# Layer norm, attention and a squared-ReLU gate on one core: another order at three borders

## The chip, the cores and the metric

The kernel runs on one core of a Trainium2 chip. The metric is the device time of one execution in microseconds (us); the median of three runs is compared. A profile is one further execution, whose span runs from the first to the last instruction.

The engines are named as the profile names them: PE (TensorE) does matmuls, PEld is its weight load, DVE is VectorE, ACT is ScalarE, POOL is GpSimd, and SP is SyncE, which here only issues DMAs. PE writes its results to PSUM, which has eight banks of 128 x 512 float32.

## The reference

```
xn = layernorm(x)                            # x: 2048 x 640
q  = xn @ wq                                 # 32 heads of 128
k, v = last 512 rows of k_cache, v_cache     # 32 heads, 512 x 128 each
p  = softmax(q @ k.T * 128**-0.5)            # per head, 2048 x 512
s  = concat(p @ v) @ wo                      # 2048 x 640
h  = relu(xn @ w1 + b1) ** 2                 # w1: 640 x 1728
g  = silu(h @ w2 + b2)                       # w2: 1728 x 640
out = x + s * g
```

Everything is float32. The kernel reaches this precision with three matmuls per product: each operand is split into a high part (rounded by ACT to the type that PE multiplies) and a low part (the rest, one subtraction), and high x high, high x low and low x high are added up in PSUM. So every operand costs one ACT operation, one DVE or POOL operation, and every 128 x 128 x 512 product three matmuls.

## The kernel before, in words

**MLP.** The 2048 tokens are four tiles of 512. F = 1728 is 13 chunks of 128 and one of 64, which stands as chunk 3. `mlp_step(n)` goes over (tile, chunk) for tiles 0 to 2: `up(t, f)` (15 matmuls, `ph`), then relu on ACT, square on POOL, the high part on ACT and the low part on DVE (`h`), and, one step later, `down` of the chunk before (15 matmuls into five banks `py`). So PE does up(f + 1) between up(f) and down(f). After a tile, `gate` writes the sigmoid gate to DRAM (`g_d`).

Tile 0 is made by `ln_first`: four blocks of x are loaded, normalised and turned by 20 PE transposes (`px`), behind 32 transposes of the identity (`pw`, `WARM`). The biases come through POOL's DMA queue (`br`) and are turned by one transpose (`pb`) that stands on PE ahead of those of x. During tile 0 the weights are read and split too: `load_w(f)` reads and splits chunk f ahead of `up(0, f)`; chunks 1 and 2 are read early into spare buffers. The statistics of tile t + 1 are made in one go at chunk 5 of tile t (`ln_stats`; chunk 3 for the last tile), its normalised chunks from chunk 9 (7) on. Instructions made through `pe`, `dve`, `act`, `pool` and `sp` keep the program's order; those made through `nc.` may be moved by the scheduler.

**Attention.** A unit is one head and one tile of 512 tokens: 128 units, in two halves of two tiles each. A hand-written plan (`at`, `on`) gives each step a due time in units of `PERIOD`; the steps are then issued in the order of these times. In unit i PE does the four score groups `s` (12 matmuls) into the four `s` banks, the query of unit i + 2 (`pq`, 15), the values of unit i - 1 (`o`, 12) and, for a finished pair of heads, the output projection (`r`, 15 per unit). The softmax of a unit: `max_fold` on DVE for each score bank (`rdm`), `gather` on ACT, `row` on DVE (`rowm`), a store of the maxima to DRAM (`m_d`) and a broadcast load of them (`bm`), both on SP; then `shift` on DVE (`e`), which empties the score banks, `expo` and `p_hi` on ACT, `p_lo` and the sum `su` on POOL. The sums take a like way (`rds`, `rows`, `s_d`, `bs`), and `o_norm`, `o_hi` and `o_lo` make `ot` from the one `o` bank. `pq` and `r` share two banks.

**Borders.** The last tile's MLP is done within attention. Its chunks 11 to 13 (`FA = FC - 3`) are multiplied by `early_up` (`eu`) in units 0 to 3, where there is no `r` yet; `late_relu`, `late_square` and `early_split` make their high and low parts, which go to DRAM (`h_d`). The other chunks run behind the last unit (`lu`, `ly`), with the three early ones last, five gates and the last stores. At the start of the second half, the two new tiles of xT are loaded in 20 pieces by SP (`load_xT`, `ax`), and each finished piece of the first half is stored at once (`s_d<-acc`).

Of the kernel before, what the change touches and what calls it, by code (L numbers as in the profile page):

```python
# [14 lines left out]
P = 128  # L15
NT = 512
EPS = 1e-5
WARM = 32
# [3 lines left out]
def kernel(  # L22
# [65 lines left out]
    h_d = {f: dpool.tile([P, 2, NT], F32, name=f"h_d{f}") for f in range(FC - 3, FC)}  # L88
# [13 lines left out]
    FA = FC - 3  # L102
# [10 lines left out]
    for f, (f0, n) in enumerate(chunks):  # L113
        wp = wpa if f < FA else wpb
        if n < P:
            w1s.append([wp.tile([P, DC, 2 * n], F32R, name=f"w1s{f}")])
        else:
            if f < FA - 1:
# [12 lines left out]
    def ln_tile(t, b):  # L131
        tag = "stage" if t or b < 2 else "mr"
        return xp.tile([P, D], F32, tag=tag, name=f"xb{t}_{b}")

    def ln_stats(t):
        mv = xp.tile([P, 4, NB], F32, tag="mv", name=f"mv{t}")[:, :2, :]
        sc = xp.tile([P, 3, NB], F32, tag="sc", name=f"sc{t}")
        sts = [
            xp.tile([P, 2, 6], F32, tag="st", name=f"st{t}_{b}", bufs=4) for b in range(NB)
        ]  # L140
        xn = []
        for b in range(NB):
# [3 lines left out]
            xn.append(xb)  # L146
        hd = D // 2
        for b in range(NB):
            for i in range(2):
                dve.bn_stats(sts[b][:, i, :], xn[b][:, i * hd : (i + 1) * hd])  # L150
            dve.bn_aggr(mv[:, :, b], sts[b])
        var, sd, y = (sc[:, i, :] for i in range(3))
        r = mv[:, 1, :]
        dve.tensor_scalar(var, r, EPS, None, op0=ALU.add)
        nc.scalar.activation(sd, var, AF.Sqrt)
# [5 lines left out]
        xs = [  # L161
            keep.tile([P, DC, NT], F32R, tag="acc", name=f"xT{t}_{i}", bufs=2)
            if t % 2
            else xp.tile([P, DC, NT], F32R, tag=f"xT{i}", name=f"xT{t}_{i}", bufs=1)
            for i in range(2)
        ]
        return mv, xs

    def ln_rows(t, mv, xs):
# [7 lines left out]
        for i in range(2):  # L177
            m = xp.tile([P, D], F32, tag="mr", name=f"mr{t}_{i}")[:, :NT]
            nc.sync.dma_start(m, d[i : i + 1, :].to_broadcast([P, NT]))
            bc.append(m)  # L180
        return bc, xs
# [9 lines left out]
    PRE = {}  # L191

    def ln_first():
# [7 lines left out]
        pool.memset(warm, 1.0)  # L201
        act.activation(warm, warm, AF.Sqrt)
# [7 lines left out]
        dve.memset(br, 0.0)  # L210
        for lo, hi in ((0, rp), (rp, rp + 1), (rp + 1, FC)):
# [4 lines left out]
        pool.dma_start(br[32 : 32 + DC, :], b2.rearrange("(c p) -> c p", p=P))  # L216
        raws = load_w_raw(0)
        PRE.update({f: load_w_raw(f, True) for f in (1, 2)})
# [3 lines left out]
        pb = ps_h.tile([P, NT], F32, tag="ph", name="pb")  # L222
        pe.transpose(pb[:, :P], br, ident)
# [15 lines left out]
        def newton(k, eng):  # L239
            sign = -1.0 if k == 0 else 1.0  # L240
            eng.tensor_tensor(R[k], Y[k], Y[k], op=ALU.mult)
            eng.tensor_tensor(R[k], R[k], VAR[k], op=ALU.mult)
            eng.tensor_scalar(R[k], R[k], -0.5 * sign, 1.5 * sign, op0=ALU.mult, op1=ALU.add)
            eng.tensor_tensor(R[k], R[k], Y[k], op=ALU.mult)
# [23 lines left out]
        newton(0, pool)  # L268
# [9 lines left out]
        split_hi(0, raws, 0)  # L278
        dve.reciprocal(Y[1], SD[1])
        newton(1, dve)  # L280
# [10 lines left out]
        dve.tensor_copy(b1_sb, pb[:, :FC])  # L291
        dve.tensor_copy(b2_sb, pb[:, 32 : 32 + DC])
        pool.tensor_copy(warm, xn[NB - 1][:, D - 1 :])
        split_lo(0, raws, 0, pool)
# [3 lines left out]
        split_hi(1, PRE[1], 0)  # L298
        split_lo(1, PRE[1], 0, pool)
        split_hi(0, raws, 1)  # L300
        split_lo(0, raws, 1, dve)
# [6 lines left out]
    def load_w_raw(f, early=False):  # L308
        f0, n = chunks[f]
        if early:  # L310
            two = keep.tile([P, 2, D], F32, tag="acc", name=f"wr{f}", bufs=2)
            wa, wb = two[:, 0, :].rearrange("p (c n) -> p c n", n=P), two[:, 1, :]
        else:
            wa = xp.tile([P, DC, P], F32, tag="stw", name=f"w1r{f}", bufs=2)
        nc.sync.dma_start(
            wa[:, :, :n], w1[:, f0 : f0 + n].rearrange("(c p) f -> p c f", p=P)
        )
        if not early:
            wb = xp.tile([P, D], F32, tag="stw", name=f"w2r{f}", bufs=2)
        for k in range(0, P, n):  # L320
            nc.sync.dma_start(wb[k : k + n, :], w2[f0 : f0 + n, :])
        return wa[:, :, :n], wb
# [7 lines left out]
    def split_hi(f, raws, k, engine=act):  # L330
        engine.activation(split_parts(f, k)[0], raws[k], AF.Copy)

    def split_lo(f, raws, k, engine):
        hi, lo = split_parts(f, k)
        engine.tensor_tensor(lo, raws[k], raw(hi), op=ALU.subtract)

    def load_w(f):
        if f == 1:
            parts = ((1, 1), (2, 0))
        elif f == 2:  # L340
            parts = ((2, 1),)
        else:
            parts = ((f, 0), (f, 1))
        raws = PRE.get(f) or load_w_raw(f)
        for m, k in parts:
            if f < 3:
                split_hi(m, PRE[m], k)
                split_lo(m, PRE[m], k, dve)
            else:
# [782 lines left out]
```

## Time and profile before

| | |
|---|---|
| runs | 1979.35, 1977.17, 1979.55 us; median 1979.35 |
| profiled execution | 1980.79 us, span 1979.0 us |
| instructions | 25665, of these 8608 matmuls |
| PE busy | 1959.6 us, 99% of the span |
| DVE, POOL, ACT busy | 77%, 70%, 60% |
| mean granted TensorE clock | 0.998 |
| DMA | 220.35 MB, 111 GB/s over the span |

Matmuls are pipelined: a row's mean time of one (about 390 ns) is longer than the distance between two starts, and the busy time of PE counts the ends as the profile models them. A loss on PE is therefore read best from how many matmuls a stretch holds against its length.

### The profile page before, as it was taken

The numbers are of one execution on the slowest core, as the hardware profiler recorded it, in microseconds if no ns is written. First come the engines' busy times: TensorE is split into PE (matmuls) and PEld (weight loads), VectorE is DVE, ScalarE is ACT, GpSimd is POOL, SyncE is SP. The second block draws the span as 40 slices with busy tenths as digits, with TensorE's granted clock in tenths as the row PEclk, the third lists the DMA queues.
The fourth block names the chain that finished last, engine by engine and source line by source line (L and its number), as shares of the span: only waits on it lengthen the run. The fifth ranks groups of instructions, "written<-read, shape, count | busy, mean of one in ns | idle before, by whom it ended". The sixth has DMA issues, their size and how long they took to land.

```text
span 1979.0 us, 25665 instructions
## 1 busy us (share of the span) xinstructions
PE 1959.6 (99%) x8608; PEld 1611.1 (81%) x8608; DVE 1530.7 (77%) x2639; ACT 1188.1 (60%) x2039; POOL 1378.9 (70%) x763
## 2 busy tenths in 40 slices
PE   9999999999999999999999999999999999999998
PEld 7888887788888888888887778888888888888887
DVE  6433337788888888888887778888888888888864
ACT  5332336766666666666665676666666666666643
POOL 2121226888888888888887778888888888888841
PEclk9999999999999999999999999999999999999999
DMA  5331453333323223323335433333333333233454
GB/s 169 105 118 27 181 198 131 102 91 93 92 93 92 91 91 91 91 91 92 93 96 165 156 99 107 112 112 113 115 110 115 114 112 113 97 91 91 110 150 139
DMA packets 128917, 220.35 MB, mean 111 GB/s; under 512 B 23590, under 2 KB 38352, under 8 KB 127504
## 3 DMA queue, kind: packets, MB, share of 16 engines
q1 hardware_dynamic: 125792, 204.28, 34.5%
q0 software_dynamic: 2992, 14.43, 1.8%
q8 instruction: 67, 1.10, 0.2%
q14 instruction: 66, 0.54, 0.1%
HBM read 194.26 MB, written 24.39 MB: 110 GB/s over the span
## 4 chain that ended last, share of the span: by engine, by line
PE 79%; DVE 7%; DMA 6%; ACT 5%; issue 2%; POOL 1%; SPq 0%; ACTq 0%; POOLq 0%; DVEq 0%
PE r L73 18%; PE pq L73 18%; PE o L73 14%; PE s L73 14%; PE ph L391 6%; DMA bm<-m_d 2%; DVE e L73 2%; DMA m_d<-rowm 2%; PE py L97 2%; PE py L98 2%; PE py L96 2%; PE ly L73 2%; ACT e L73 1%; DVE rdm L73 1%; DVE acc L73 1%
## 5 line engine op out<-in xcount | busy, mean ns | idle before, releaser
L73 POOL TENSOR_TENSOR pt<-e,pt 128x1024 fp32r<-128x1024 f32 x256 | 616.4, 2408 | 130.8 <-ACT pt L73 105.0
L73 PE MATMUL r<-ot,wo 128*128 128x512 f32 x1920 | 497.0, 389 | 0.2 <-DVE acc L73 0.2
L73 PE MATMUL pq<-ax,wq 128*128 128x512 f32 x1920 | 456.5, 389 | 0.9 <-DMA ax<-xT_d 0.8
L73 PEld LDWEIGHTS pq<-ax,wq 128*128 128x128 f32 x1920 | 360.4, 188 | 76.3 <-DMA ax<-xT_d 1.7
L73 PEld LDWEIGHTS r<-ot,wo 128*128 128x128 f32 x1920 | 360.2, 188 | 75.8 <-DVE acc L73 0.6
L73 PE MATMUL s<-q,wk 128*128 128x512 f32 x1536 | 370.3, 390 | 5.0 <-DVE e L73 5.0
L73 PE MATMUL o<-pt,wv 128*128 128x512 f32 x1536 | 372.5, 391 | 2.0 <-DVE ot L73 1.4
L73 ACT ACTIVATE e<-e 128x1024 f32<-128x1024 f32 x256 | 269.7, 1053 | 140.6 <-DVE e L73 119.1
L73 DVE TRANSPOSE_TENSOR_REDUCE rdm<-s 128x16 f32<-128x512 f32 x512 | 342.8, 707 | 1.4 <-PE s L73 1.3
L73 PEld LDWEIGHTS s<-q,wk 128*128 128x128 f32 x1536 | 287.6, 188 | 68.3 <-DVE e L73 8.2
L73 PEld LDWEIGHTS o<-pt,wv 128*128 128x128 f32 x1536 | 286.8, 188 | 68.0 <-DVE ot L73 5.0
L73 DVE TENSOR_TENSOR e<-s,bm 128x512 f32<-128x512 f32 x512 | 312.6, 666 | 22.4 <-DMA bm<-m_d 22.2
L73 POOL TENSOR_TENSOR su<-e,e 128x1024 f32<-128x1024 f32 x128 | 308.0, 2406 | 0.0
L73 ACT ACTIVATE pt<-e 128x1024 fp32r<-128x1024 f32 x256 | 271.8, 1062 | 7.8
L73 DVE TENSOR_TENSOR acc<-r,acc 128x512 f32<-128x512 f32 x300 | 203.0, 677 | 8.8 <-PE r L73 8.5
L354 POOL TENSOR_TENSOR r<-r 128x512 f32<-128x512 f32 (+1 forms) x42 | 44.1, 1049 | 209.9 <-ACT r L399 190.9
L73 ACT ACTIVATE ot<-o 128x512 fp32r<-128x512 f32 x128 | 76.7, 599 | 172.3 <-DVE o L73 172.3
L73 DVE TRANSPOSE_TENSOR_REDUCE rds<-su 128x32 f32<-128x1024 f32 x128 | 158.3, 1237 | 1.6 <-POOL su L73 1.6
L73 DVE TENSOR_TENSOR ot<-o,ot 128x512 fp32r<-128x512 f32 x128 | 88.6, 692 | 85.2 <-ACT ot L73 85.2
L391 PE MATMUL ph<-xT,w1s 128*128 128x512 f32 x585 | 139.3, 390 | 0.0
L73 ACT ACTIVATE q<-pq 128x512 fp32r<-128x512 f32 x128 | 76.7, 599 | 101.2 <-PE pq L73 100.9
L73 POOL TENSOR_TENSOR wq<-qr,wq 128x640 fp32r<-128x640 f32 x62 | 97.8, 1577 | 56.5 <-ACT wq L73 56.5
(131 smaller groups left out, 2026.5 us busy)
## 6 DMA issues: line engine op xcount, KB each, us to landing
bm<-m_d SPq DMA_DIRECT2D x128, 256.0 KB, 3.3
bs<-s_d SPq DMA_DIRECT2D x128, 256.0 KB, 3.9
qr<-in_wq_dram SPq DMA_DIRECT2D x64, 320.0 KB, 4.3
or<-in_wo_dram SPq DMA_DIRECT2D x64, 320.0 KB, 4.2
kr<-in_kT_dram SPq DMA_DIRECT2D x64, 256.0 KB, 3.3
vr<-in_v_dram SPq DMA_DIRECT2D x64, 256.0 KB, 4.2
xT_d<-xT POOLq DMA_DIRECT2D x6, 1280.0 KB, 7.5
xb<-in_x_dram SPq DMA_DIRECT2D x16, 320.0 KB, 3.3
```

The lines of the kernel that those rows point to most:

```text
L73: ins = method(*args, **kwargs)
L96: nc.tensor.matmul(ps, ah, bh, start=first and i == 0, stop=False)
L97: nc.tensor.matmul(ps, ah, bl, start=False, stop=False)
L98: nc.tensor.matmul(ps, al, bh, start=False, stop=last and i == n - 1)
L354: nc.gpsimd.tensor_tensor(r, r, r, op=ALU.mult)
L391: nc.tensor.matmul(ph, w1s[f][i][:, c, :], xs[j][:, c, :], start=k == 0, stop=k == len(order) - 1,)
```

## The change

- **Start and first tile.** `WARM` is 36. The bias loads go through SP, behind the two weight loads of chunk 0, and `biases()` turns them behind the tenth matmul of `up(0, 0)`. `root` takes the square root with the epsilon as its bias; `newton` has three DVE steps for the second pair of blocks. `load_part(f, k)` reads w1 (k = 0) or w2 (k = 1) of a chunk two chunks ahead up to chunk 9, one ahead after that. `split_w(f, 1)` stands ahead of `up(0, f)`, `split_w(f + 1, 0)` behind the square of chunk f. Tile 0 uses the ordered engines. The statistics of tile 1 are loaded at chunk 1, made at chunks 2 to 5 (`ln_block`), and finished by `ln_var` and `ln_root`.
- **Border to attention.** `FA = FC - 4`: chunk 10 is done early as well. Its product stands where the query of unit 1 stood, and that query goes into unit 0 with the one of unit 2. `early_square` squares from PSUM in one operation; the square alone goes to DRAM, and `late_hs` splits it at the end.
- **Units.** The second `p_hi` stands behind the next unit's gather. From unit 4 on, `o` of even units uses the spare bank.
- **Border between the halves.** `load_xT` is issued by ACT at other times, `store_acc` is a step of its own one to three units later. `finish` is cut into `finish_gate` and `finish`.

The core of the diff:

```
-WARM = 32
+WARM = 36
...
-    FA = FC - 3
+    FO, FA = FC - 3, FC - 4
...
-            pool.dma_start(
+            sp.dma_start(
                 br[lo:hi, :m], b1[f0 : f0 + m * (hi - lo)].rearrange("(f p) -> f p", p=m)
             )
...
-        pb = ps_h.tile([P, NT], F32, tag="ph", name="pb")
-        pe.transpose(pb[:, :P], br, ident)
...
         def root(k):
+            act.activation(SD[k], R[k], AF.Sqrt, bias=eps)
             dve.tensor_scalar(VAR[k], R[k], EPS, None, op0=ALU.add)
-            act.activation(SD[k], VAR[k], AF.Sqrt)
...
+    def split_w(f, k):
+        if f < FC:
+            split_hi(f, PRE[f, k], k)
+            split_lo(f, PRE[f, k], k, dve)
+            if 9 <= f < FC - 1:
+                load_part(f + 1, k)
...
+    def square_split(t, f, r, hi, lo):
+        g, a, v = engines(t)
+        g.tensor_tensor(r, r, r, op=ALU.mult)
+        if t == 0 and f:
+            split_w(f + 1, 0)
+        a.activation(hi, r, AF.Copy)
+        v.tensor_tensor(lo, r, raw(hi), op=ALU.subtract)
...
+            if t == f == 0 and k == 9:
+                biases()
...
             if t == 0 and f > 0:
-                load_w(f)
+                split_w(f, 1)
+                if f < 8:
+                    for k in range(2):
+                        load_part(f + 2, k)
...
-            QPS[i] = bank(f"pq{i}", int(i != 1))
+            QPS[i] = bank(f"pq{i}", 1)
...
-            PO[i] = pools["psb"].tile([P, NT], F32, tag="o", name=f"o{i}", bufs=1)
+            if i % 2 or i < UPG:
+                PO[i] = pools["psb"].tile([P, NT], F32, tag="o", name=f"o{i}", bufs=1)
+            else:
+                PO[i] = psx.tile([P, NT], F32, tag="x", name=f"o{i}")
...
-        if g == NG - 1 and hf == 0:
-            sp.dma_start(s_d[t][:, d, :], ACC[hf, t][:, d, :])
+
+    def store_acc(t, d):
+        sp.dma_start(s_d[t][:, d, :], ACC[0, t][:, d, :])
...
+    def early_square(f):
+        r = LR[f]
+        dve.scalar_tensor_tensor(
+            r, LPH.pop(f), b1_sb[:, f : f + 1], r, op0=ALU.add, op1=ALU.mult
+        )
...
-    q_mm(1, range(DC))
-    q_hi(1)
-    q_lo(1)
+    EARLY_IN = (-1,) * 5 + (0,) * 4 + (1,) * 4 + (2,) * 4 + (3,) * 3
+    EARLY = [(FA + n // DC, n % DC) for n in range(len(EARLY_IN))]
+    for (f, c), u in zip(EARLY, EARLY_IN):
+        if u < 0:
+            early_up(f, 0, c)
...
-            w = (NG * UPG + t * G - 3 - AHEAD + t + k) * PERIOD + (8.5 if late else -1.6)
...
+        w = (NG * UPG + t * G - 5) * PERIOD
+        X_AT = [(11.65, 2)]
+        for k in (1, 2):
+            X_AT += [(k * PERIOD + 3.97, 2), (k * PERIOD + 7.85, 1)]
+            X_AT += [(k * PERIOD + 11.65, 2)] * (k == 1)
...
+                at(w + when, load_xT, 1, t, i, slice(c, c + 1), act)
...
+        qs = [(i + AHEAD, 3.45 if i % G and i > UPG else 4.3, 4.1)]
+        if i == 0:
+            qs = [(1, 2.8, 4.1), (2, 9.1, PERIOD - 5.2)]
+        elif i < UPG:
+            qs = [(i + 2, 4.9 if i == 3 else 4.2, 4.1)]
...
-        on(14.8, p_hi, i, 1)
+        on(PERIOD + 4.0, p_hi, i, 1)
...
-    EARLY_IN = (0,) * 7 + (1,) * 3 + (2,) * 3 + (3,) * 2
```

More of the change, by code (lines that the diff above doesn't have):

```diff
@@ L160, in ln_stats, with ln_rows @@
         dve.tensor_tensor(r, r, y, op=ALU.mult)
[L161 to L169, printed above, removed]
+        return mv
+    def ln_rows(t, mv):
         pm = psx.tile([P, NT], F32, tag="x", name=f"pmv{t}")
@@ L180, in ln_rows @@
             bc.append(m)
+        xs = [
+            keep.tile([P, DC, NT], F32R, tag="acc", name=f"xT{t}_{i}", bufs=2)
+            if t % 2
+            else xp.tile([P, DC, NT], F32R, tag=f"xT{i}", name=f"xT{t}_{i}", bufs=1)
+            for i in range(2)
+        ]
         return bc, xs
@@ L306, in spill, with load_part @@
             pool.dma_start(xT_d[t][i][:, cs, :], raw(xs[i])[:, cs, :])
[L308 removed]
+    def load_part(f, k):
         f0, n = chunks[f]
[L310 to L322 removed]
+        if f % 3 and f < 9:
+            if k == 0:
+                BOTH[f] = keep.tile([P, 2, D], F32, tag="acc", name=f"wr{f}", bufs=2)
+            w = BOTH[f][:, k, :]
+        else:
+            w = xp.tile([P, D], F32, tag="stw", name=f"w{k + 1}r{f}", bufs=2)
+        if k == 0:
+            w = w.rearrange("p (c n) -> p c n", n=P)[:, :, :n]
+            sp.dma_start(w, w1[:, f0 : f0 + n].rearrange("(c p) f -> p c f", p=P))
+        else:
+            for i in range(0, P, n):
+                sp.dma_start(w[i : i + n, :], w2[f0 : f0 + n, :])
+        PRE[f, k] = w
     def split_parts(f, k):
```

246 lines of the change are left out of this document (134 added, 112 removed).

## The prediction

> **What bounds the kernel now.** I read the page first, then the busy times by stage (with the matmul counts in brackets behind PE), then what the tensor engine (PE) waited for, then the timelines of the places where it lost time.
>
> ```profile
> span 1979.0 us, 25665 instructions
> ```
> ```profile
> 0.00:13.40 13.40, 10.00 (x53) 9.78 (x54) 7.62 (x28) 6.67 (x12) 4.81 (x17) 0.87 0.87 272
> 13.40:70.00 56.60, 55.49 (x241) 43.83 (x240) 34.45 (x58) 30.04 (x48) 10.91 (x10) 1.00 0.54 151
> 70.00:300.00 230.00, 230.00 (x1017) 189.67 (x1016) 78.26 (x139) 73.95 (x112) 49.59 (x61) 1.00 0.33 119
> 300.00:376.00 76.00, 72.96 (x312) 57.45 (x311) 56.59 (x96) 50.93 (x91) 54.47 (x36) 1.00 0.39 125
> 376.00:1038.00 662.00, 662.00 (x2921) 548.05 (x2920) 579.40 (x997) 438.58 (x763) 540.32 (x272) 1.00 0.31 92
> 1038.00:1160.00 122.00, 117.36 (x499) 92.24 (x498) 95.23 (x168) 75.16 (x132) 90.19 (x47) 1.00 0.50 149
> 1160.00:1900.00 740.00, 739.74 (x3262) 611.08 (x3261) 640.09 (x1108) 487.05 (x850) 612.60 (x313) 1.00 0.36 108
> 1900.00:1979.00 79.00, 72.07 (x317) 59.03 (x315) 39.10 (x51) 25.76 (x39) 16.02 (x12) 0.98 0.49 154
> ```
>
> Columns: stretch, its length, then busy time and count of PE, its weight loads, DVE, ACT and POOL, the granted clock, DMA share, GB/s. The stretch 376 to 1038 has no idle PE: 662.00 us for 2921 matmuls, 0.22663 us each. That is the floor of a matmul here, and it turns each row into a loss, length minus count x 0.22663. First tile (13.4 to 70): 56.60 - 54.62 = 1.98. From 70 to 300: nothing. Border to attention (300 to 376): 76.00 - 70.71 = 5.29. Border between the attention halves (1038 to 1160): 122.00 - 113.09 = 8.91. From 1160 to 1900: 0.73. Tail: 79.00 - 71.84 = 7.16, nearly all of it the gate and store after the last matmul. Ahead of the first real matmul stand 13.40. The change leaves the number of 512-wide matmuls alone, so it can move these 37 us and no others; without its three stalls the span would be near 1963.
>
> **The change part by part.**
>
> *Start.* Rows of the timeline (start, length), a stage row, a row of the DMA issues (its last number: us from issue to landing):
>
> ```profile
> 1.52 2.23 POOL L73 DMA_DIRECT2D br<-in_b_dram  x4 [0.16 <-issue]
> ...
> 7.71 0.83 ACT L73 ACTIVATE xb<-xb,mv 128x640 f32<-128x640 f32 x1 [0.64 <-POOL mv L73]
> 8.08 0.89 DVE L73 BATCH_NORM_STATS2 st<-xb 128x6 f32<-128x320 f32 x2 [0.88 <-DMA xb<-in_x_dram]
> ...
> 9.65 4.01 PE L73 MATMUL px<-ident,xb 128*128 128x128 f32 x20
> ...
> 17.52 0.69 ACT L399 ACTIVATE r<-ph,b_sb 128x512 f32<-128x512 f32 x1 [0.46 <-PE ph L391]
> ```
> ```profile
> 9.74:13.16 3.42, 3.42 (x18) 3.41 (x17) 2.61 (x12) 2.07 (x4) 0.82 (x2) 0.50 1.00 340
> ```
> ```profile
> br<-in_b_dram POOLq DMA_DIRECT2D x1, 2.5 KB, 6.1
> ```
>
> The last of the four bias loads was issued near 3.2 and landed 6.1 later, at 9.3. Its transpose stood on PE ahead of the 20 transposes of x, though the first x block was scaled at 7.71 + 0.83 = 8.54. The twenty then ran without a gap at a granted clock of 0.50, so they are on the path. The change puts the bias transpose behind the tenth matmul of chunk 0, puts the bias loads behind two weight loads on SP, takes one small DVE operation from ahead of each root and one of the last four Newton steps (0.4 us in all), and adds four warm-up transposes. The transposes can start 9.65 - 8.54 = 1.1 sooner and the first matmul with them, at 12.3; bounds 13.4, and 11.4 if block 3 of x, for which DVE idled 0.88, lands sooner without POOL's queue beside it. A new wait takes some back: the bias copies now stand on DVE behind the splits of xT and of w2, so the first relu (17.52) comes less than 1.1 sooner, and the first down matmuls hang on it. I take 0.9; bounds 2.0, and -0.9 if the clock stays at 0.50 for the first four matmuls (4 x 0.227). The bias loads themselves are issued by 6, land by 12.1 even at 6.1, and are wanted ten matmuls after 12.3, at 14.5.
>
> The Trainium skill ("TensorE: Matmul & The Clock Gate", Part 1: The HAM clock gate) says that the activity window is free-running and 3413 ns long; the 3.42 us row at 0.50 agrees.
>
> *First tile.* Rows of the PE waits (us in total, times, longest), then of the timeline:
>
> ```profile
> PE s L73 <- DVE e L73: 5.0, 8, 1.1
> ...
> PE pq L73 <- DMA ax<-xT_d: 0.8, 1, 0.8
> PE py L96 <- ACT h L355: 0.5, 1, 0.5
> PE py L97 <- DVE h L356: 0.4, 1, 0.4
> ```
> ```profile
> 42.60 0.74 ACT L331 ACTIVATE w1s<-w1r 128x640 fp32r<-128x640 f32 x1 [1.27 <-DMA w1r<-in_w_dram]
> ```
>
> ACT idles for a weight load (1.27) while the squared activations queue behind it, and PE then waits for h. A read two chunks ahead has 2 x 30 x 0.227 = 13.6 us of PE time to land. The fixed order puts the next chunk's w1 split into the time of POOL's square. Statistics go to one block per chunk, 0.9 and a little of DVE, where the stage has 56.6 - 34.5 = 22 idle: nothing, or 0.9 at most in one chunk without that cover. The two waits give 0.9, the slow restarts after them the rest: I take 1.3, bounds 0 and 2.0.
>
> *Border to attention.* PE and DVE timelines:
>
> ```profile
> 308.58 4.92 PE L73 MATMUL eu<-xT,w1s 128*128 128x512 f32 x21
> 313.76 3.00 PE L73 MATMUL s<-q,wk 128*128 128x512 f32 x12 [0.26 <-DVE e L73]
> ...
> 326.08 3.04 PE L73 MATMUL s<-q,wk 128*128 128x512 f32 x12 [0.99 <-DVE e L73]
> ```
> ```profile
> 322.44 1.71 DVE L73 TENSOR_TENSOR eh_g<-lr,eh_x 128x512 fp32r<-128x512 f32 x1
> ...
> 325.39 2.43 DVE L73 TENSOR_TENSOR e<-s,bm 128x512 f32<-128x512 f32 x4
> ```
>
> A unit's four score banks are freed by the shift (e), which waits for the round trip of the maxima through DRAM. Until then PE needs other work: a steady unit has 54 matmuls (12.24 us), units 0 to 2 have 48 (10.9). The change moves chunk 10 (15 matmuls, 3.4 us) from the tail to here, neutral in count, and gives unit 0 54 matmuls, units 1 and 2 51, unit 3 54. PE was ready for unit 1 at 308.58 + 21 x 0.227 = 313.3; with six matmuls more it is ready at 314.7, after the bank came free (by 313.76): no stall. The hi/lo split of the early chunks, 1.71 us of DVE ahead of the shift of 325.39, goes to the tail, where DVE is busy 39 of 79 us and covers four of 0.6 (2.43 / 4); uncovered they cost 2.4. I take 4.5; bounds 5.3, and 2.4: units held by DVE at 326.08 - 313.76 = 12.3 take in the 15 matmuls and gain just 3.4, less one more wait of 1.0.
>
> *Border between the halves.* SP and DVE timelines, the DMA issues, and one early issue on SP:
>
> ```profile
> 1038.80 0.93 SPq L73 DMA_DIRECT2D ax<-xT_d  x2
> 1042.94 0.32 SPq L73 DMA_DIRECT2D m_d<-rowm  x1
> 1046.67 0.32 SPq L73 DMA_DIRECT2D bm<-m_d  x1
> ```
> ```profile
> 1050.19 2.48 DVE L73 TENSOR_TENSOR e<-s,bm 128x512 f32<-128x512 f32 x4 [1.99 <-DMA bm<-m_d]
> ```
> ```profile
> m_d<-rowm SPq DMA_DIRECT2D x128, 2.0 KB, 1.3
> ```
> ```profile
> 5.65 2.73 SPq L321 DMA_DIRECT2D wr<-in_w_dram  x1
> ```
>
> The 2 KB store of the maxima took 1046.67 - 1042.94 = 3.7 where 1.3 is usual: large loads stood in the same queue, the two of the first row last. A delay of 2.4 is more than the steady slack of 1.5 (below). The change issues the 20 loads of xT from ACT and ends them, by the planned times, 3 us sooner; the ten stores of the first half go behind the issue of bm, and the gather goes ahead of the second p_hi. I take 7.0 of the 8.91; bounds 8.9, and 1.5 as in rival (a). ACT now issues DMAs with the exponentials queued behind them, and no row shows an issue on ACT. On SP one took 0.32 to 0.47 here, 2.73 at worst (last row). A steady unit shows the cover (ACT, POOL, DVE, PE):
>
> ```profile
> 649.76 0.79 ACT L73 ACTIVATE rdm<-rdm 32x64 f32<-32x64 f32 x3 [0.58 <-DVE rdm L73]
> ```
> ```profile
> 651.97 2.42 POOL L73 TENSOR_TENSOR pt<-e,pt 128x1024 fp32r<-128x1024 f32 x1
> ```
> ```profile
> 656.21 2.43 DVE L73 TENSOR_TENSOR e<-s,bm 128x512 f32<-128x512 f32 x4
> ```
> ```profile
> 648.11 1.06 ACT L73 ACTIVATE pt<-e 128x1024 fp32r<-128x1024 f32 x1
> ```
> ```profile
> 654.25 2.88 PE L73 MATMUL o<-pt,wv 128*128 128x512 f32 x12
> ...
> 658.33 2.88 PE L73 MATMUL s<-q,wk 128*128 128x512 f32 x12
> ```
>
> The first shift ends near 656.8 and the next scores start at 658.33: slack 1.5. The second low part ends at 654.39 and is wanted by the eighth matmul of o, 654.25 + 7 x 0.227 = 655.84: slack 1.45. With p_hi behind the gather, p_hi ends at 649.76 + 0.79 + 1.06 = 651.6, 0.36 before POOL wants it. Two issues of 0.43 fit into both: nothing. At t per issue a pair ahead of an exponential costs 2t - 1.45, a pair after a gather 2t - 1.81.
>
> *The rest.* Even units keep o in the spare bank, which ends the waits for ot beyond 1160 (part of 0.73), and a fourth chunk in the last group spaces the gates by 2.72 instead of 2.04. I take 0.6, bounds 0 and 1.2.
>
> Sum: 0.9 + 1.3 + 4.5 + 7.0 + 0.6 = 14.3. The profiled execution took 1980.79 (its span and 1.8 around it), 1.44 above the median of 1979.35. Expected: profiled 1966.5, median 1965.0.
>
> **The rivals.**
>
> (a) It is not the queue that delays the maxima but the 16 engines behind it. Then 20 loads of 256 KB cost m_d and bm the same from ACT, and only the wait for ax goes (0.8, with two restarts 1.5). For it: x block 3 came late at the start beside another queue. Against: the stage moves 149 GB/s where 9.74 to 13.16 moves 340. Gain 14.3 - 5.5 = 8.8: 1970.5.
>
> The Trainium skill ("DMA: Bandwidth & Descriptors", Issuing engines are not separate DMA queues) says that the same 16 engines serve every issuer, so that spreading saves issue time alone; that is this rival. Its section Queues, rings and completion order has each engine take turns between the queues, which would let a 2 KB store past a backlog; that is the forecast. No row here has two hardware queues busy at once.
>
> (b) Slower: ACT is held by its issues. The eight pairs cost 4 x (2t - 1.45) + 4 x (2t - 1.81) = 16t - 13.0. At t = 2.73 that is 30.6, net 16.3 slower: 1995.6. It decides from t = 1.7, where it eats the 14.3. For it: SP shows an issue of 2.73. Against: that one came amid the loads of the start (340 GB/s), and near the border the rows stay under 0.5.
>
> (c) Start, first tile and first units give back what they gain (bias copies late, SP's order keeping reads late, DVE holding units at 12.3): the second border and the rest remain, 7.6: 1971.8.
>
> **How the numbers follow.** Forecast 0.65, (a) 0.15, (b) 0.10, (c) 0.10. About 0.2%, 4 us, is what a measurement of this kernel can tell from no change. Forecast, (a) and (c) lie beyond it but for 0.04, mixtures of (a) and (c) that end within it. So faster 0.86, same 0.04, slower 0.10. All upper bounds together give 19.4, all lower 3.0; neither is likely, and 1960.5 (18.9) to 1973.0 (6.4) holds the forecast, (a) and (c).
>
> **What would show it.** First ph near 12.3; no idle of ACT for w1r after 20 us; s starting 12.24 apart from unit 0, units 1 and 2 under 12; m_d to bm below 2.5 us in units 60 to 67; losses by the same floor of about 0.8 and 1.9 in the two borders. Wrong if s still starts within 0.1 us of the end of e there, if ACT shows idle at its DMA issues, or if a new wait appears behind the first relu.

## The result, and the profile after

The changed kernel takes 1966.49 us (median of 6 runs, 1966.04 to 1967.65); the kernel before, run beside it, 1978.80 (6 runs, 1977.17 to 1980.40). The ratio is 0.9939, 95% interval 0.9926 to 0.9952: faster by 12.3 us, where the prediction had 14.35 and a median of 1965.0. The profiled execution took 1966.04 and spans 1964.2 us, 14.8 less than before. On the chips of the later experiments the kernel before is itself quicker (medians 1974.5 to 1976.0) and the changed one is not (1966.53), so that the gain there is 9.5; where the profiled executions differ is shown below.

The busy times of the changed kernel by stage; columns as in the prediction:

```profile
0.00:13.40 13.40, 9.37 (x57) 8.65 (x58) 8.00 (x27) 7.42 (x13) 2.97 (x13) 0.91 0.83 267
13.40:70.00 56.60, 56.52 (x246) 45.62 (x246) 30.79 (x52) 24.58 (x40) 11.17 (x11) 0.99 0.38 116
...
300.00:376.00 76.00, 75.97 (x335) 62.58 (x335) 56.69 (x97) 51.78 (x91) 55.41 (x35) 1.00 0.38 118
376.00:1038.00 662.00, 661.61 (x2917) 546.84 (x2916) 576.86 (x996) 437.56 (x761) 539.25 (x271) 1.00 0.31 92
1038.00:1160.00 122.00, 121.08 (x528) 98.38 (x527) 100.14 (x176) 79.48 (x143) 96.58 (x49) 1.00 0.49 152
1160.00:1900.00 740.00, 740.00 (x3266) 612.62 (x3265) 641.04 (x1107) 484.70 (x841) 608.02 (x312) 1.00 0.36 109
1900.00:1964.20 64.20, 58.11 (x257) 47.80 (x255) 35.40 (x43) 22.15 (x33) 11.45 (x8) 0.97 0.49 155
```

Length minus count x 0.22663 is again the loss. First tile 56.60 - 55.75 = 0.85 (1.98 before). Border to attention 76.00 - 75.92 = 0.08 (5.29). Border between the halves 122.00 - 119.66 = 2.34 (8.91). From 1160 to 1900 nothing (0.73). Tail 64.20 - 58.24 = 5.96 (7.16). One row is worse: 376 to 1038 loses 0.9 where it lost nothing; that is a single stop of unit 19, taken up at the end. The waits of PE, which before had eight for the shift:

```profile
PE px L73 <- ACT xb L73: 2.5, 1, 2.5
...
PE s L73 <- DVE e L73: 1.1, 3, 0.6
```

The waits for ax and for h (py) are gone. The start gave little. Its timeline:

```profile
6.83 0.49 DVE L73 BATCH_NORM_STATS2 st<-xb 128x6 f32<-128x320 f32 x1 [0.79 <-DMA xb<-in_x_dram]
7.24 0.15 DVE L73 RECIPROCAL sc<-sc 128x2 f32<-128x2 f32 x1
...
8.53 0.83 ACT L73 ACTIVATE xb<-xb,mv 128x640 f32<-128x640 f32 x1 [1.65 <-POOL mv L73]
...
9.41 3.93 PE L73 MATMUL px<-ident,xb 128*128 128x128 f32 x20 [2.52 <-ACT xb L73]
...
13.00 3.25 PE L411 MATMUL ph<-xT,w1s 128*128 128x512 f32 x10
...
20.74 0.39 PE L96 MATMUL py<-h,w2s 128*128 128x512 f32 x1
```
```profile
11.06:14.47 3.41, 3.41 (x15) 2.95 (x14) 2.99 (x7) 2.80 (x6) 1.69 (x2) 0.50 1.00 352
```

The transposes of x start at 9.41 instead of 9.65, when block 0 is scaled (8.53 + 0.83 = 9.36), and they run with gaps. The granted clock is 0.50 from 11.06 to 14.47 (second fence, a stage row), so the first matmuls of ph are slow too. The first down matmul (L96) stands at 20.74, where it stood at 20.72.

The second border, unit 60, on the queues of ACT and SP, then the shift on DVE:

```profile
1039.12 0.33 ACTq L73 DMA_DIRECT2D ax<-xT_d  x1
1039.49 0.44 ACTq L73 DMA_DIRECT2D ax<-xT_d  x1
...
1043.12 0.60 ACT L73 ACTIVATE q<-pq 128x512 fp32r<-128x512 f32 x1 [0.94 <-PE pq L73]
1043.12 0.33 ACTq L73 DMA_DIRECT2D ax<-xT_d  x1
```
```profile
1040.37 0.32 SPq L73 DMA_DIRECT2D m_d<-rowm  x1
1043.51 0.33 SPq L73 DMA_DIRECT2D bm<-m_d  x1
```
```profile
1047.71 2.48 DVE L73 TENSOR_TENSOR e<-s,bm 128x512 f32<-128x512 f32 x4 [2.09 <-DMA bm<-m_d]
```

The store of the maxima still takes 1043.51 - 1040.37 = 3.14, with SP free of the loads of xT. So the second border is better, but a store that has none of these loads in its queue is still held. The runs below look for the reason.

### The profile page after: what moved, and what is told of

It reads as the page before. It is cut to its first block, busy times and chain, and to the rows that moved or that the text cites. A ratio compares the mean times of both kernels' runs of the same rounds, so it can differ in the third digit from the quotient of the medians.

```text
span 1964.2 us, 25621 instructions
## 1 busy us (share of the span) xinstructions
PE 1952.7 (99%) x8612; PEld 1612.2 (82%) x8612; DVE 1535.0 (78%) x2640; ACT 1186.1 (60%) x2038; POOL 1375.1 (70%) x757
## 5 line engine op out<-in xcount | busy, mean ns | idle before, releaser
L73 ACT ACTIVATE rdm<-rdm 32x64 f32<-32x64 f32 x384 | 97.7, 254 | 173.9 <-DVE rdm L73 170.7
L73 POOL TENSOR_TENSOR wv<-vr,wv 128x512 fp32r<-128x512 f32 x64 | 83.1, 1298 | 71.4 <-ACT wv L73 64.3
```

The source lines that it names most:

```text
L73: ins = method(*args, **kwargs)
```

## The experiments

Every kernel below ran beside the kernel before on its chip. The table shows where their profiled executions spent the time (us, from the starts of matmuls in the timelines). "First down" is the start of the first down matmul, with the stretch at clock 0.50 noted; "first tile" runs from there to the first up matmul of tile 1; "units 0-5" and "units 60-69" run from scores to scores (the floor of ten units is 540 x 0.22663 = 122.4); "end" runs from the scores of the last unit to the start of the last matmul. Chunk 10 moves 15 matmuls, 3.40 us, from "end" to "units 0-5".

| kernel | first down | first tile | units 0-5 | units 60-69 | end |
|---|---|---|---|---|---|
| before | 20.72 (0.50) | 85.30 | 74.35 | 131.61 | 103.80 |
| before, again | 19.11 | 85.00 | 73.60 | 127.69 | 102.96 |
| start and first tile alone | 18.97 | 83.83 | 73.75 | 128.57 | 103.04 |
| first border alone | 19.89 | 84.42 | 72.45 | 126.13 | 99.56 |
| second border alone | 20.77 (0.50) | 84.63 | 73.44 | 125.93 | 103.16 |
| queue alone | 20.01 | 84.99 | 74.21 | 129.27 | 104.39 |
| changed | 20.74 (0.50) | 83.55 | 72.41 | 125.05 | 99.56 |
| changed, again | 19.51 | 83.83 | 72.40 | 124.53 | 99.56 |
| changed, loads on SP | 19.37 | 83.87 | 72.40 | 127.35 | 99.56 |
| changed, loads behind exp | 19.72 | 83.89 | 72.45 | 126.00 | 99.56 |
| changed, loads behind splits | 19.75 | 83.89 | 72.45 | 124.33 | 99.56 |
| changed, maxima on ACT | 20.11 | 83.84 | 72.40 | 140.52 | 99.56 |
| changed, 44 warm-ups | 19.61 | 83.90 | 73.78 | 125.18 | 99.56 |
| changed, behind splits and 44 | 19.75 | 83.91 | 73.41 | 122.88 | 99.56 |

### The start and the first tile alone

Into the kernel before go the new order of the start, the reads two chunks ahead, the fixed order of steps and the spread statistics; both borders stay old.

```diff
-WARM = 32
+WARM = 36
...
+            if t == f == 0 and k == 9:
+                biases()
...
+            if t == 0 and 2 <= f < 2 + NB:
+                ln_block(1, f - 2)
```

> The kernel before with only the new start and first tile (warm-up of 36, bias loads on SP and their transpose behind the tenth matmul, weights two chunks ahead, ordered engines, spread statistics). The prediction's terms say 2.2 us less (0.9 for the start, 1.3 for the first tile): about 1976.6. The trace of the changed kernel says that the first tile alone gained: its first down matmul stood at 20.74 against 20.72, the first scores at 300.73 against 302.46, so 1.7 less, all between 20 and 106 us, and nothing after the first scores. Rival (c): nothing, 1978.8.

Measured: 1973.56 against 1975.27, ratio 0.9991 (0.9981 to 1.0000). The first tile gains 1.5 on the profile of before. With the clock at full rate the start shows the wait that the prediction expected behind the first relu (timelines of PE, then of ACT):

```profile
8.35 3.29 PE L73 MATMUL px<-ident,xb 128*128 128x128 f32 x20 [0.37 <-ACT xb L73]
11.39 3.06 PE L411 MATMUL ph<-xT,w1s 128*128 128x512 f32 x10
...
18.97 0.39 PE L96 MATMUL py<-h,w2s 128*128 128x512 f32 x1
19.39 0.50 PE L97 MATMUL py<-h,w2s 128*128 128x512 f32 x1
```
```profile
16.14 0.69 ACT L73 ACTIVATE r<-ph,b_sb 128x512 f32<-128x512 f32 x1 [1.88 <-DVE b_sb L73]
```

The first relu waits for the copies of the biases (b_sb) and not for its product; so it does in all eight profiles that have the new start at full clock. On PE this shows at the second down matmul, which follows the first by 0.42 instead of 0.23: 0.2 given back. The part as a whole is worth 1.7 in the median (0 to 3.8 by the interval), at the edge of what these runs can tell from nothing.

### The first border alone

Into the kernel before go chunk 10 in front, the new counts of units 0 to 3, and the square and store of the early chunks without their split.

```diff
+    EARLY_IN = (-1,) * 5 + (0,) * 4 + (1,) * 4 + (2,) * 4 + (3,) * 3
...
+        if i == 0:
+            qs = [(1, 2.8, 4.1), (2, 9.1, PERIOD - 5.2)]
```

> The kernel before with only the border to attention changed (chunk 10 done early, the queries of units 1 and 2 in unit 0, squares from PSUM, their split at the end). Prediction: 4.5 less there and part of 0.6 at the end. The two traces: the first six units 1.94 shorter with 15 matmuls (3.40) more in them, everything behind the last unit's scores 4.88 shorter with 15 fewer, in sum 6.8 less: about 1972. Rival, that the units are held by DVE at 12.3 us: 3.4 less. If the spare bank for o or the later p_hi is what made the six units 12.24 long, this kernel, which has neither, shows units 4 and 5 near 12.7 still.

Measured: 1967.68 against 1975.27, ratio 0.9958 (0.9943 to 0.9973): 7.6 us, the largest part. Its stage row:

```profile
300.00:376.00 76.00, 75.97 (x336) 62.52 (x335) 57.10 (x97) 52.38 (x91) 55.68 (x35) 1.00 0.36 118
```

336 matmuls in 76.00 leave no loss, as in the changed kernel. Units 4 and 5 take 12.25 and 12.24 although this kernel has neither the spare bank nor the later p_hi, so these are not needed for that. The first border and its chunk account for about 5 of the 7.6, less work at the end for half a microsecond. What the rest is isn't shown; in the profiled execution the old second border happened to lose only 126.13 - 122.4 = 3.7.

### The second border alone

Into the kernel before go the times of the loads of xT, their queue, the ten stores at times of their own and the divided finish; the spare bank for o and the later p_hi are not in it.

```diff
-            w = (NG * UPG + t * G - 3 - AHEAD + t + k) * PERIOD + (8.5 if late else -1.6)
+        w = (NG * UPG + t * G - 5) * PERIOD
...
+                at(w + when, load_xT, 1, t, i, slice(c, c + 1), act)
...
+    def store_acc(t, d):
```

> The kernel before with only the second border changed (loads of xT from ACT at the new times, stores of the first half as steps of their own, the last steps cut in two); neither the spare bank for o nor the later p_hi. Prediction: 7.0 less; the traces of both kernels: scores of unit 60 to those of unit 70 take 125.0 instead of 131.6, so 6.6 less, about 1972. Rival (b), ACT held by its issues: slower than before, or at least less than 3 gained, with idle POOL ahead of the low parts; with p_hi ahead of the gather it would show as a later gather. Rival (a): about 1.5.

Measured: 1972.33 against 1975.27, ratio 0.9983 (0.9973 to 0.9992): 2.9 us, not 7.0. The border still loses 125.93 - 122.4 = 3.5, of which 2.5 in units 60 to 63 and 1.1 in units 64 to 69. The changed kernel, which has the spare bank and the later p_hi too, loses 2.2 to 2.8; whether these two give the difference of about 1 was not tried. The three parts give 1.7, 7.6 and 2.9, in all 12.2, each with an interval 4 to 6 us wide; the whole change without ACT's queue gave 8.5 on this chip (next run).

### The loads of xT back on SP, at the new planned times

```diff
-                at(w + when, load_xT, 1, t, i, slice(c, c + 1), act)
+                at(w + when, load_xT, 1, t, i, slice(c, c + 1))
```

> The changed kernel with one edit: the 20 loads of xT go back to SP's queue, at the new times and in the new pieces. If the queue is what delays the maxima, the second border (scores of unit 60 to unit 70) goes back from 125.0 towards 131.6, by 3 us or more, and the time from 1966.5 to about 1970. Rival (a), that the 16 engines are what delays them and only the times helped: within 1 us of the changed kernel.

Measured: 1966.82 against 1975.27, ratio 0.9955 (0.9940 to 0.9969). The border of its profile is longer by 2.2 to 2.8 than in the three profiles of the changed kernel's border (125.05, 124.53, 125.18), nearly all of it in units 60 to 63; the time is the same within the intervals, which are near 6 us wide and can't tell 2 us. The edit also does more than change the queue. SP issues in order, behind its own waits, and sends the loads at other moments than ACT did (unit 60, SP's queue):

```profile
1034.44 1.82 SPq L73 DMA_DIRECT2D ax<-xT_d  x4
1038.04 0.32 SPq L73 DMA_DIRECT2D m_d<-rowm  x1
1041.95 0.32 SPq L73 DMA_DIRECT2D bm<-m_d  x1
```

Four loads go out together in the 3.6 us ahead of the store of the maxima, where ACT sent two. So this run doesn't part the queue from the place of the loads.

### The queue alone, and the changed kernel beside it

```diff
-                at(w + 0.7 * i, load_xT, 1, t, i, slice(c, c + 1))
+                at(w + 0.7 * i, load_xT, 1, t, i, slice(c, c + 1), act)
```

> The kernel before with one edit: the twenty loads of xT for the second attention half are issued from ACT instead of SP, at the old planned times. In the kernels that kept the old border, units 60 to 70 took 131.6 (the first profile), 128.6 and 126.1 us, floor 122.4. Theory 1 (the forecast: the queue holds the 2 KB store of the maxima): m_d to bm falls below 2.5 us in units 60 to 67, the stretch ends near 124, the time falls by 3 to 5. Rival (a) (the 16 engines hold it): m_d to bm stays at 3 to 4 in several units, the stretch stays within 126 to 131, the time moves by less than 1.5. Rival (b) (ACT held by its issues): ACT shows idle at its DMA issues and the time rises.

Measured: 1977.08 against 1975.99, ratio 1.0005 (0.9996 to 1.0014): nothing gained, though twenty loads left SP. (They moved in time as well: ACT sent them in groups of four, 8 to 11 us into a unit, where SP had spread them.) Unit 62, SP's queue and ACT's:

```profile
1066.14 0.32 SPq L73 DMA_DIRECT2D m_d<-rowm  x1
1070.18 0.33 SPq L73 DMA_DIRECT2D bm<-m_d  x1
```
```profile
1058.48 0.44 ACTq L73 DMA_DIRECT2D ax<-xT_d  x1
```

The store took 1070.18 - 1066.14 = 4.04 with none of the loads of xT in its queue. ACT's issues took 0.33 to 0.63 and it shows no idle at them: rival (b), which needs 1.7 for each, is out.

> The changed kernel itself, on the chip of the kernels beside it. With the loads of xT on SP at the new times it measured 1966.8 against a before of 1975.3 (0.9955). If the queue is worth anything once the times are the new ones, this kernel is below 0.9955 by 0.001 or more; if the engines behind the queues decide, it is within 0.0007 of it. Units 60 to 70 near 125 in its profile by either.

Measured: 1966.53, ratio 0.9952 (0.9939 to 0.9964), against 0.9955 with the loads on SP. The expectation put the line at 0.0007; the difference is 0.0003. By the medians nothing is seen of the queue, but two ratios from two chips, with intervals 0.0025 and 0.0029 wide, could hide some 2 us.

### Loads behind the exponentials

```diff
-        X_AT = [(11.65, 2)]
-        for k in (1, 2):
-            X_AT += [(k * PERIOD + 3.97, 2), (k * PERIOD + 7.85, 1)]
-            X_AT += [(k * PERIOD + 11.65, 2)] * (k == 1)
+        X_AT = [(k * PERIOD + when, 2) for k in range(3) for when in (11.75, 13.85)]
+        X_AT = X_AT[1:] if t else X_AT[:-1]
```

> The changed kernel, with the loads of xT moved again, still on ACT: four in each of five half units, all planned right behind the exponentials of a unit (11.75 and 13.85), so that ACT issues them in the first 2 us of the next unit, ahead of the store of the maxima at +4.9 and none between that store and the load of bm. Rival (a), engines: the loss of this border falls from 2.65 above its floor of 122.4 to 1 or less, m_d to bm under 2 us in units 60 to 64, time 1.5 to 2.5 below the changed kernel. The forecast's theory, queue alone: SP's queue is as free as it was, so the stretch stays near 125 and the time within 0.7 of the changed kernel. Rival (c) of its own kind: loads later than before reach q late, PE waits for ax, and the time rises by 1 or more.

Measured: 1966.55, ratio 0.9953 (0.9940 to 0.9965), border 126.00. The engines theory had expected stores under 2 us and a time 1.5 to 2.5 lower, and missed; the time is the one that the queue theory had named. No load is issued between store and bm, and still the store waits in unit 61 (ACT's queue, SP's queue, the DMA queues between the two SP rows; the last column is the share of 16 engines):

```profile
1046.92 0.81 ACTq L73 DMA_DIRECT2D ax<-xT_d  x2
1048.12 0.81 ACTq L73 DMA_DIRECT2D ax<-xT_d  x2
```
```profile
1052.31 0.33 SPq L73 DMA_DIRECT2D m_d<-rowm  x1
1055.77 0.33 SPq L73 DMA_DIRECT2D bm<-m_d  x1
```
```profile
q10 hardware_dynamic: 296, 0.53, 39.6%
q1 hardware_dynamic: 230, 0.38, 28.3%
```

q10 is ACT's queue, q1 SP's. Four loads of 256 KB issued by 1049 were still moving 0.53 MB after 1052.3, next to SP's own weight loads. So the expectation took the time of issue for the place of a transfer, and what counts by this reading is the bytes still in flight. The reading came after the result; the two runs that follow test it.

### The maxima on ACT's queue, the loads on SP's

```diff
-        sp.dma_start(d, r)
+        queue = act if what == "m" and 59 <= i < 67 else sp
+        queue.dma_start(d, r)
...
-                at(w + when, load_xT, 1, t, i, slice(c, c + 1), act)
+                at(w + when, load_xT, 1, t, i, slice(c, c + 1))
```

(The load of bm takes the same queue as its store.)

> The changed kernel, with the queues the other way round in units 59 to 66: the loads of xT go back to SP at their new times, and the store of the maxima and the load of bm go out from ACT, where nothing else is queued. On SP with the same times the border took 127.35, m_d to bm 3.9, 3.4, 3.9, 2.6 in units 60 to 63. Queue theory: alone in its queue the 2 KB store passes the backlog, m_d to bm 1.3 to 1.7 in these units, border 122.4 to 123.5 (up to 1 more where ACT waits for the store ahead of its next work). Engines theory: the packets stand behind those of SP on the same 16 engines, m_d to bm 2.5 to 3.9, border 125 to 128 and more, since ACT now stands behind the store too.

Measured: 1979.61 against 1974.99, ratio 1.0024 (1.0014 to 1.0033), border 140.52. ACT's timeline in units 59 and 61, and SP's queue between the two issues of unit 61:

```profile
1026.48 0.35 ACTq L73 DMA_DIRECT2D m_d<-rowm  x1
1027.85 0.35 ACTq L73 DMA_DIRECT2D bm<-m_d  x1
...
1054.33 0.33 ACTq L73 DMA_DIRECT2D m_d<-rowm  x1
1058.93 0.34 ACTq L73 DMA_DIRECT2D bm<-m_d  x1
1059.31 0.60 ACT L73 ACTIVATE ot<-o 128x512 fp32r<-128x512 f32 x1 [4.37 <-DMA m_d<-rowm]
```
```profile
q1 hardware_dynamic: 816, 1.50, 85.1%
```

This decides that a queue of its own doesn't free the store. In unit 59, with no other transfer beside it, it took 1.37 there; in unit 61, again alone in its queue, 4.60, while SP's queue moved 1.50 MB. The loads of SP don't stand where they stood in the earlier run with loads on SP, so what the store takes beyond its 3.4 there isn't the price of the queue either. ACT, which now waits for the store itself, stood idle for 4.37: that is what waiting ahead of a DMA costs an engine with work behind it.

The store's own packets came late. DMA queues from 1054.3 to 1056.9, in which q10 has no row, and q10's from 1056.9 to 1058.5:

```profile
q1 hardware_dynamic: 552, 1.04, 104.1%
```
```profile
q10 hardware_dynamic: 48, 0.00, 1.9%
```

The first of the 48 packets moved 2.6 us after the issue; in a unit with free engines (20 of the kernel before) it is 0.8.

All fourteen profiles together say the same. Take the stores of units 6 to 125 without an instruction packet (last section) in their first 1.3 us, and count what other transfers started in these 1.3 us. With under 0.02 MB, 1248 stores have a median of 1.34. With 0.4 to 0.6 MB from the store's own queue alone, 21 stores have 2.90 (2.06 to 4.04). With as much from another queue alone, 9 stores have 2.32 (2.13 to 4.60). Bytes from either queue delay it; whether those of its own queue cost somewhat more stays open.

### Loads behind the splits of the weights

```diff
+        X_AT = [(k * PERIOD + when, n) for k in range(3) for when, n in ((9.6, 3), (11.75, 1))]
+        X_AT = [(11.75, 2)] + X_AT[2:] if t else X_AT[:4] + [(2 * PERIOD + 9.6, 2)]
```

> The changed kernel, the twenty loads of xT once more moved, on ACT: in units 59 to 63 three behind the splits of the weights (9.6) and one behind the first exponential (11.75). The measured ones behind the exponentials moved some 1.6 MB (four pieces and SP's own weight loads) from +0.3 of a unit to +9 and so lay across the store of the maxima at +5. These go out 2 us earlier, when the load of bm has landed (+9.8) and the engines stand at 68 GB/s. Engines theory: most is moved by +5; m_d to bm 2.5 or less in units 60 to 64, this border 123 to 124.3 (loss 0.6 to 1.9 of the 2.1 to 2.7 left), the time 0.5 to 2 below the changed kernel. If it is the number of bytes per unit and not their place: m_d to bm 2.9 to 3.5 as behind the exponentials, 126, no gain. Queue theory: no change, 125.

Measured: 1963.42 against 1974.99, ratio 0.9939 (0.9927 to 0.9952), border 124.33. Units 60 and 61, SP's queue:

```profile
1038.42 0.33 SPq L73 DMA_DIRECT2D m_d<-rowm  x1
1040.47 0.33 SPq L73 DMA_DIRECT2D bm<-m_d  x1
1050.67 0.33 SPq L73 DMA_DIRECT2D m_d<-rowm  x1
1052.72 0.33 SPq L73 DMA_DIRECT2D bm<-m_d  x1
```

2.05 in both, and neither unit stops; 62 and 64 still do (3.13 and 3.49), where 2.5 or less was expected. The same number of bytes per unit as behind the exponentials, two microseconds earlier, costs 1.7 less in one execution of each. That speaks for the place and not the number, as the engines theory has it, but the three profiles of the changed kernel's border alone differ by 0.6.

### 44 warm-ups, alone and with the moved loads

```diff
-WARM = 36
+WARM = 44
```

> The changed kernel with 44 instead of 36 warm-up transposes, so that PE goes on until about 7.8 instead of 6.9 us and idles less ahead of the transposes of x. Theory (the clock at 0.50 over one window of 3.4 us cost the start its gain in the profile of after): the granted clock stays at 1.00 to 15 us, the first ph comes at 11.4 to 12.0, and the time falls by 0.3 to 0.9. Rival: the windows of the clock fall as they like, the clock drops here too in some runs, and the time stays within 0.3. Other side: where PE starts cold, the warm-ups end near 8.8 and hold the transposes of x by 0.5: 0.5 slower.

Measured: 1965.77, ratio 0.9952 (0.9938 to 0.9965). The clock stays at 1.00, but so it did in six of the seven profiles with the new start and 36: no gain shown.

> The changed kernel with both small edits: loads of xT behind the splits of the weights, and 44 warm-up transposes. Behind the splits alone: 1963.4, ratio 0.9939 [0.9927, 0.9952], border of 124.33; 44 warm-ups alone: 0.9952 [0.9938, 0.9965]. If the places of the loads are what gave the 3 us in the median, the ratio is at or below 0.994, and m_d to bm is again short in units 60 and 61 (2.1) with a stop in 62 and 64. If that was the spread between sets of runs (the border of the profile was 124.53 in the changed kernel and 124.33 there), the ratio falls at 0.995 like the changed kernel's own. The warm-ups keep the clock at 1.00 over the first 16 us; worth nothing where it stays there without them.

Measured: 1964.43 against 1974.51, ratio 0.9946 (0.9933 to 0.9960), border 122.88, in which one unit stops for half a us (unit 59, just ahead of it, for another 0.28). This and the 0.9939 of the moved loads alone lie within the intervals of the changed kernel's own two ratios (0.9939 and 0.9952). This one profile says that the second border can be all but emptied; that the time falls by more than the spread between sets of runs is not shown.

### The kernel before once more

> The kernel before once more, for its profile on another chip. On the first chip its median was 1979, on others 1975 to 1976, the changed kernel 1966.5 on all. If the second border is what varies: units 60 to 70 take 126 to 129 here instead of 131.6, and the other intervals stay within 1 us of the first profile. If the start is: the first down matmul comes near 19.9 instead of 20.7, with the clock at 1.00.

Measured: a profiled execution of 1973.32, 7.5 less than the first. Both vary: 3.9 of it is the second border (127.69 instead of 131.61), 1.6 the start (first down matmul at 19.11, clock at 1.00), and the other three intervals give 0.3 to 0.8 each. The profile from which the prediction was worked out was a dear one in both places. What makes the border differ from one execution to the next, and whether the chip has a part in it, stays open.

## Why the prediction was right, and where it was not

The total was right: 14.8 less in the profile (14.3 forecast), 12.3 in the median (14.35). Its terms, in the order of the sum:

**Start, 0.9.** Mis-sized. In the profile after it is nothing by the first down matmul; over all profiles the old start has a mean of 20.10 (five) and the new one 19.74 (seven with 36 warm-ups), 0.4. Where the clock stayed at 1.00 they stand at 19.67 (three) and 19.57 (six). The step that failed is that the first matmul moves with the first transpose. At full clock the first ph follows the end of the scale of block 0 by 3.21 in all three executions with the old start, whether the bias transpose had held the twenty (8.98 behind a scale at 8.45, in the kernel before once more) or not (9.29 behind 9.23, with the first border alone). With the new start it follows by 3.09 to 3.11 in five of six. Transposes that start sooner wait for the later blocks instead. And the bias transpose in its new place adds 0.13 between the first ph and the first down matmul (7.58 instead of 7.45). The scale itself came hardly sooner either (8.89 in the mean of the seven, 9.01 in that of the five): it needs the reciprocal, which stands on DVE behind the statistics of block 2, and in the profile after that block landed late (6.83), so the scale ended at 9.36 and the first ph came at 13.00, not 12.3.

What moves the start most is the clock: 20.7 in the three executions with a stretch at 0.50, 19.0 to 20.1 in the others. The rule cited there (the Trainium skill, "TensorE: Matmul & The Clock Gate", Part 1: The HAM clock gate) has a free-running window: the trace agrees, the 0.50 lasted 3.41 again and began at 11.06 instead of 9.74.

**First tile, 1.3.** Right: 1.75 in the profile, 1.0 by the means (84.87 in five profiles with the old order, 83.83 in nine with the new). ACT no longer idles for w1r after 20 us.

**Border to attention, 4.5.** Right in mechanism; 5.2 in the profile, the upper end. By the means (five profiles with the old border, seven with the new, the two at 73.4 and 73.8 left out) it is 3.40 + 73.87 - 72.42 = 4.85; with these two it is 4.6. Scores start 12.24, 11.89, 11.56 and 12.24 apart in units 0 to 3, as forecast (12.24, units 1 and 2 under 12). DVE does not hold the units at 12.3.

**Border between the halves, 7.0.** The number held in this profile (6.6), its first reason did not, and that the two met is luck. The step that failed is "large loads stood in the same queue": the queue alone gave nothing (1.0005), and a store alone in a queue took 4.60. What holds the store is what the 16 engines have in flight, the mechanism of rival (a). But (a) priced it wrongly: it took the cost of twenty loads as fixed, so that only the wait for ax would go. What helped are the new times of the loads and of the stores of acc, which the prediction named beside the queue. In the first profile units 64 to 69 lost 4.9 of the 9.2 (they took 13.96, 12.70, 12.86, 13.48, 13.08 and 12.24). The last loads of xT went out in unit 64, and two of the ten stores of acc stood ahead of the maxima in unit 67, whose store of the maxima took 4.24 (kernel before, SP's queue):

```profile
1133.15 2.44 SPq L73 DMA_DIRECT2D s_d<-acc  x2
1136.02 0.32 SPq L73 DMA_DIRECT2D m_d<-rowm  x1
1140.26 0.32 SPq L73 DMA_DIRECT2D bm<-m_d  x1
```

In the changed kernel the loads end by unit 63, the stores of acc go out behind the load of bm, and these units lose 0.4 (12.60 in unit 64). They lose 0.5 with the loads on SP too, so ACT's queue is not needed for it. Over four profiles with the old loads on SP and three with the changed kernel's, units 64 to 69 went from a mean loss of 3.6 to 0.2, and units 60 to 63 only from 2.5 to 2.3: the gain is the first of these. The kernel with the queue alone helps to part it. Its loads, too, ended in unit 63, and its stores of acc are the old ones: in its one profile unit 64 loses nothing and units 65 to 69 lose 2.8. So the larger part seems to be the stores of acc.

The size 6.6 (8.91 to 2.34) also belongs to one execution: the four profiles lie between 126.13 and 131.61, mean 128.5, the three at 124.53 to 125.18, mean 124.9. That is 3.6. It fits a gain of 12.3 beside one set of runs of before and of 9.5 beside another, but one profile of before on each of two chips can't show that this is the cause.

The two rules set against each other there can be settled in part. The Trainium skill ("DMA: Bandwidth & Descriptors", Issuing engines are not separate DMA queues) has all issuers on the same 16 engines: the runs agree. Its section Queues, rings and completion order has turns between queues, on which the forecast leaned; no turn let the store past, whose first packet moved 2.6 us after its issue. The same section also says that the semaphore increment of a transfer lands only after every earlier write of that engine, across its queues. The trace leaves little of the 4.60 to that: the store's last packet was done by 1058.41, 0.52 ahead of the issue of bm, against 0.36 in the free unit. Why the packets themselves come late stays open.

**The rest, 0.6.** Low. The stretch from unit 70 to 126 gave 0.75, the end beyond the moved chunk 103.80 - 3.40 - 99.56 = 0.84, and what follows the last matmul 7.15 - 6.51 = 0.64, in all 2.2 in this profile. By the means of the profiles with the old end and the new (five and nine) the last two are 0.5 each and the first is nothing: 1.0, inside the bounds.

Of the signs that things go as forecast: the loss of the two borders was to be about 0.8 and 1.9, and is 0.08 and 2.34. The store was to stay below 2.5 in units 60 to 67; it does but in 60 (3.14) and 62 (2.51). The scores start within 0.06 of the end of the shift in two units, 60 and 61, which is the sign against the mechanism, on a small scale. The new wait behind the first relu did appear (0.2 on PE). ACT did show idle at its issues: three times p_hi started 0.20 to 0.75 late behind an issue of 0.51 to 1.06, for which PE shows no wait. Unit 19 took back 1.1 of the profile's gain. By the means the terms are 0.4, 1.0, 4.85, 3.6 and 1.0, in all near 10.8, between the 9.5 and the 12.3 of the medians.

## What to carry to other kernels

Before pricing the gain of removing a stall, ask whether the stall is the same in another execution: this one lay between 3.7 and 9.2 us in four executions with the same code at that border, and one profile showed the dear end. A small transfer on the critical path was delayed here by what the engines had in flight, from any queue; give it an empty window by counting the bytes issued in the 5 us ahead of it, and don't expect another queue to free it. Moving a transfer to another issuer also moves its time of issue, so such a run tests two things. Removing one wait ahead of a row of work gains nothing where the end of the row waits for something else, as with the first transposes here. The stall made by the order of compute (the first border) varied by 0.9 us and could be worked out to half a microsecond.

## What the runs showed of the hardware

**Many stores beside an instruction packet are slow.** Unit 19 of the changed kernel, SP's queue and the DMA queues between its two rows:

```profile
537.56 0.33 SPq L73 DMA_DIRECT2D m_d<-rowm  x1
541.26 0.33 SPq L73 DMA_DIRECT2D bm<-m_d  x1
```
```profile
DMA packets 49, 0.02 MB, mean 5 GB/s; under 512 B 48, under 2 KB 48, under 8 KB 48
q8 instruction: 1, 0.02, 1.6%
```

The store took 3.70 on engines that moved almost nothing but one instruction packet of 16 KB. Count the stores of units 6 to 57 and 72 to 125 in all fourteen profiles by what lies in their first 1.3 us. Without a packet of an instruction queue the median is 1.34 in 1192 stores, and 20 of them are over 2.0. With a 16 KB packet of q8 it is 1.99 in 129 stores, and 64 are over 2.0. With an 8 KB packet of q14 alone it is 1.35 in 163. A packet of q8 lies also beside the store of unit 0 (3.41 and 3.12) in the two executions whose units 0-5 took a microsecond more (73.78 and 73.41). That the packet is the cause was not tried by itself. These stops come at other units in other executions; the one of unit 19 cost 1.1 us.

**Issuing from ACT cost little.** An issue takes 0.33 at least, 1.06 at most in the changed kernel, and starts while the ACTIVATE ahead of it still runs (both at 1043.12 in the fence of unit 60). The longest delayed a p_hi by 0.75. It is dear where ACT has to wait for the data of the transfer first: 4.37 in the kernel with the maxima on ACT.
